# New assumed times in the planner that orders the first batch of an attention and MoE kernel

## The chip, the cores and the metric

The kernel runs on one core of one Trainium2 chip. The metric is the device time of one execution in microseconds; executions of one kernel lie within about half a per cent of their median.

Engine names in the profile: PE is TensorE, PEld its weight loads, ACT is ScalarE, DVE is VectorE, POOL is GpSimd, SP is SyncE.

## The reference

Eight batches of attention with a bias that depends on the distance of query and key, then one MoE-like block on the result:

```python
# q, k, v: (8, 8, 576, 64); bias_table: (32, 8); w_in: (512, 2048); w_out: (2048, 512)
scores = q @ k.T / sqrt(64) + bias[head, bucket(|i - j|)]
attn   = exp(scores - max) / sum            # softmax
x      = (attn @ v), heads side by side     # (4608, 512)
h      = x @ w_in
g      = h + sin(alpha * h)**2 / (alpha + 1e-9)
out    = g @ w_out                          # float32
```

## The kernel before

The kernel does not emit instructions in source order. It describes its work as tasks, each with its engines, an assumed length, its dependencies and an earliest time `nb`. A list scheduler then plays the program through with these assumed times, and emits each task at the moment at which it "starts" in that play. The assumed times therefore decide the *order* of instructions on each engine, and nothing else: on the chip every engine waits on semaphores for its real inputs. Its core:

```python
def ready(self, t):
    r = t.nb                                  # assumed earliest time
    ...                                       # + ends of dependencies, + buffers that come free
def run(self, t0):
    ...
    for t in todo:                            # cut: windows, priorities
        st = max(free[e], self.ready(t))
    ...                                       # the earliest start wins
    t.emit(e)                                 # the instruction is written HERE, in this order
    t.end, t.eng = fin + LAT[e], e
```

The constants that stand for measured times, in us:

```python
T_M2 = (16.8, 20.0)    # landing of the bias factors "m2r" (first head pair, other pairs)
T_MH = (18.0, 18.0)    # landing of the tail factors "mhr"
T_TR1 = (33.0, 37.0)   # landing of "nat", the staged keys and queries of the second batch
T_W = 30.0             # w_in
```

The first batch works on four head pairs p = 0 to 3. For each: scores on PE (`qk`), exponentials on ACT (`ex`), multiplication by the bias factors on DVE (`bd`, `bh`), the products with v on PE (five groups of nine products), normalising on DVE (`norm`), a transpose on PE (`turn`) and a copy into `xT` (`put`, on DVE or ACT). When all four pairs are in `xT`, the first MoE block starts with its sines on ACT. For the second batch, keys and queries are transposed on PE from the staged copy `nat`:

```python
def plan_tr(t, p, kq, pri, nb, deps=()):
    def mm(e):
        c.v = bank("moE").bitcast(F16)
        ...                                   # 12 transposes that read nat2[:, kq, h, ...]
    m = plan.add({"PE": 0.4 if t == 0 and p == 0 else 0.5}, mm, deps, pri, nb, new=[b])
...
if t == 0:
    for p in range(NP):
        for kq in range(2):
            tr[(1, p, kq)] = plan_tr(1, p, kq, 20000 + 100 * kq + 10 * p, T_TR1[kq])
```

The loads come from POOL's queue, in a fixed order that the planner does not touch:

```python
load_m2r(P_, 0, 2)
load_mhr(P_)
cast_v(0, P_, (0, 1))
load_m2r(P_, 2, H)
load_w_in16((0,))
cast_v(0, P_, (2, 3, 4, 5))
load_w_in16((1, 2, 3))
for kq, src in ((0, k), (1, q)):
    load_nat(nat2[:, kq], 0, H, src[1], P_)   # nat
load_v32(1, P_)
load_w_out16()
```

The softmax here doesn't subtract the row's maximum and nothing guards it: scores larger than these inputs give would overflow.

## Time and profile before

| | before |
|---|---|
| time, 6 executions | median 392.96 us (392.29 to 393.67) |
| profiled execution, span | 392.2 us |
| PE busy | 378.4 us, 96% |
| last exponential of the first batch ends | 33.5 us |
| first sine starts | 39.09 us |
| second batch's table load (exponentials may start) | 55.78 us |

The page of the kernel before, its part on busy engines:

```profile
PE 378.4 (96%) x3401; PEld 190.1 (48%) x3401; DVE 262.0 (67%) x587; ACT 323.9 (83%) x458; POOL 81.9 (21%) x96
```

The windows view of the kernel before; each line is one stretch (start:end, length), then busy time of PE, PEld, DVE, ACT and POOL, the granted clock of PE, the DMA share and GB/s.

```profile
22.72:26.13 3.41, 2.00 (x22) 1.21 (x24) 3.35 (x11) 2.63 (x4) 2.63 (x3) 1.00 1.07 211
26.13:29.54 3.41, 3.41 (x46) 2.40 (x46) 2.22 (x7) 2.25 (x4) 0.88 (x1) 0.50 1.06 214
20.00:41.00 21.00, 18.00 (x281) 12.11 (x281) 14.36 (x49) 14.79 (x21) 10.11 (x15) 0.92 1.12 211
57.00:80.00 23.00, 22.99 (x302) 13.30 (x302) 15.80 (x45) 22.18 (x31) 5.57 (x4) 1.00 1.94 166
```

From 57 to 80 us PE is full, and the same view gives it 237.95 busy us of the 240 us from 80 to 320. Nearly all slack is in the first batch, and there one stretch of 3.41 us ran at half clock. Part of the chain of waits of the kernel before (start, length, what):

```profile
15.74 6.42 DMA m2r<-e_dram
22.16 0.02 issue
22.18 0.42 DVE u L730
...
23.36 0.34 PE am L822 x3
```

The second head pair's bias factors land late, DVE starts on them at 22.18, and the first transpose of PE (L822) waits behind DVE. This is what the change aims at. PE's timeline of the kernel before where the first batch ends (start, length, engine, line, operation, output and inputs, shapes, count, and in brackets the idle time ahead with what ended it):

```profile
34.04 0.29 PE L822 MATMUL ca<-id_sb,xn 128*128 128x128 f16 x2 [0.25 <-DVE xn L785]
34.30 0.22 PE L450 MATMUL am<-vh,u 128*128 128x130 f16 x1
...
35.80 0.81 PE L450 MATMUL sc<-xT,w_in 128*128 128x512 f16 x3
...
39.63 0.45 PE L558 MATMUL am<-id_sb,nat 96*64 96x96 f16 x12
```

The last pair's products with v (`am<-vh,u`) start at 34.30, the MoE block's products (`sc<-xT,w_in`) at 35.80, and the first transposes of `nat` come at 39.63, long after `nat` has landed. ACT's timeline of the same stretch:

```profile
33.55 1.28 ACT L937 ACT_TABLE_LOAD   x1
...
39.09 1.84 ACT L865 ACTIVATE s<-sc,alphaT 128x512 f16<-128x512 f32 x3 [1.18 <-PE sc L450]
...
55.78 1.28 ACT L937 ACT_TABLE_LOAD   x1
```

From 39.09 to 55.78 us ACT is full with the block's sines and squares.

### The profile page before, as it was taken

To read this page: it belongs to the slowest core of one execution; us is meant where nothing else is said; L and a number is where in the kernel's file an instruction comes from. 1 tells how busy PE (TensorE), PEld (TensorE's weight loads), DVE (VectorE), ACT (ScalarE), POOL (GpSimd) and SP (SyncE) were. 2 spreads that over 40 slices of the span, in tenths; PEclk is the share of its full clock that TensorE was granted. 3 is DMA by queue.
4 is the path that set the end of the run, shared out by engine and by line. 5 is a ranking of instruction groups with operands and counts; after the bars stand their busy time and mean duration, and the time that the engine had idled before them with its cause. 6 is when DMAs were issued, how large, how long until landed. Compare 5 with 4: busy or idle time off the path is not lost.

```text
span 392.2 us, 8566 instructions
## 1 busy us (share of the span) xinstructions
PE 378.4 (96%) x3401; PEld 190.1 (48%) x3401; DVE 262.0 (67%) x587; ACT 323.9 (83%) x458; POOL 81.9 (21%) x96
## 2 busy tenths in 40 slices
PE   6989999999999999999999999999999999999995
PEld 2456445644455554445445544554445444444442
DVE  3576987768576689567967895768676869429100
ACT  2976999979899999999989999999999969539211
POOL 5762963090004545001700310000000000000000
PEclk9989999999999999999999999999999999999999
DMA  9999999999726999991996497211014000020122
GB/s 170 211 204 219 207 171 158 166 171 148 92 59 83 158 155 157 158 166 47 150 170 101 34 93 166 68 33 42 27 43 59 17 28 29 27 80 2 57 76 80
DMA packets 148647, 41.99 MB, mean 107 GB/s; under 512 B 137784, under 2 KB 142992, under 8 KB 148608
## 3 DMA queue, kind: packets, MB, share of 16 engines
q0 software_dynamic: 89872, 19.04, 56.9%
q1 hardware_dynamic: 58512, 22.36, 30.3%
q8 instruction: 26, 0.43, 0.5%
q14 instruction: 13, 0.11, 0.1%
q10 hardware_dynamic: 224, 0.05, 0.1%
HBM read 37.76 MB, written 16.52 MB: 138 GB/s over the span
## 4 chain that ended last, share of the span: by engine, by line
PE 86%; DMA 4%; DVE 4%; ACT 3%; POOL 1%; issue 1%; ACTq 0%; DVEq 0%
PE sc L450 41%; PE am L450 34%; PE cb L450 5%; PE ca L450 5%; ACT u L705 2%; DMA m2r<-e_dram 2%; DMA e_dram<-e_sb 1%; DMA phi_sb<-phi_const 1%; DVE g L879 1%; DVE u L730 1%; ACT s L865 1%; DVE xn L785 1%; DVE outs L538 0%; DVE kT L538 0%; POOL mhr L471 0%
## 5 line engine op out<-in xcount | busy, mean ns | idle before, releaser
L705 ACT ACTIVATE u<-sc 128x1024 f16<-128x1024 f32 (+1 forms) x192 | 157.8, 898 | 14.4 <-PE sc L450 12.9
L450 PE MATMUL sc<-xT,w_in 128*128 128x512 f16 x576 | 132.3, 379 | 0.6 <-DVE g L879 0.5
L879 DVE SCALAR_TENSOR_TENSOR g<-sq,inv_a,sc 128x512 f16<-128x512 f16 x144 | 103.3, 746 | 22.1 <-PE am L450 14.7
L450 PE MATMUL am<-w_out,g 128*128 128x512 f16 x416 | 108.6, 380 | 0.3 <-DVE outs L538 0.2
L865 ACT ACTIVATE s<-sc,alphaT 128x512 f16<-128x512 f32 x144 | 92.7, 678 | 6.4 <-PE sc L450 5.0
L730 DVE TENSOR_TENSOR u<-u,m2r 128x512 f16<-128x512 f16 (+2 forms) x160 | 67.7, 438 | 32.4 <-ACT u L705 27.8
L450 PEld LDWEIGHTS <-w_in 128*128 128x128 f16 x576 | 55.3, 98 | 65.0 <-issue 1.3
L450 PEld LDWEIGHTS <-g 128*128 128x128 f16 x576 | 53.3, 98 | 64.1 <-issue 11.6
L450 PEld LDWEIGHTS <-u 128*128 128x128 f16 x1440 | 55.8, 98 | 19.2 <-issue 11.0
L450 PE MATMUL sc<-qT,kT 64*128 64x64 f16 (+1 forms) x512 | 50.8, 297 | 1.7 <-ACT u L705 0.9
L450 PE MATMUL am<-v,u 128*128 128x65 f16 x1152 | 51.2, 194 | 0.0
L872 ACT ACTIVATE sq<-s 128x512 f16<-128x512 f16 x79 | 49.2, 628 | 2.2 <-DVE g L879 0.5
L396 POOL DMA_DIRECT2D v<-in_v_dram x24 | 22.2, 1065 | 119.6 <-PE am L450 104.3
L874 DVE TENSOR_TENSOR sq<-s 128x512 f16<-128x512 f16 x65 | 27.4, 423 | 9.2 <-ACT s L865 8.8
L450 PE MATMUL am<-vh,u 128*128 128x130 f16 x144 | 32.2, 224 | 0.8 <-DVE xp L785 0.8
L450 PEld LDWEIGHTS <-kT 64*128 64x128 f16 x512 | 14.7, 96 | 28.5 <-issue 24.3
L785 DVE TENSOR_TENSOR xp<-am,rd 128x384 f16<-128x384 f32 (+1 forms) x48 | 23.6, 491 | 1.8
L784 DVE RECIPROCAL rd<-am 128x6 f32<-128x6 f32 (+1 forms) x56 | 10.5, 187 | 19.7 <-PE am L450 19.2
L450 PE MATMUL cb<-w_out,g 128*128 128x512 f16 x96 | 23.0, 380 | 0.0
L937 ACT ACT_TABLE_LOAD x13 | 16.7, 1283 | 0.2
L377 POOL DMA_DIRECT2D staged_q<-in_q_dram x6 | 15.5, 2583 | 3.6 <-DMA staged_q<-in_q_dram 3.6
L538 DVE COPY outs<-am 128x512 f32<-128x512 f32 x19 | 13.1, 688 | 4.3 <-PE am L450 4.1
(88 smaller groups left out, 175.6 us busy)
## 6 DMA issues: line engine op xcount, KB each, us to landing
out_dram<-outs SPq DMA_DIRECT2D x36, 256.0 KB, 2.2
staged_k<-in_k_dram POOLq DMA_DIRECT2D x6, 576.0 KB, 13.8
staged_q<-in_q_dram POOLq DMA_DIRECT2D x6, 576.0 KB, 19.7
v<-in_v_dram POOLq DMA_DIRECT2D x24, 128.0 KB, 7.0
w_in<-in_moe_w_in_dram POOLq DMA_DIRECT2D x4, 512.0 KB, 8.8
w_out<-in_moe_w_out_dram POOLq DMA_DIRECT2D x4, 512.0 KB, 10.7
w_out<-in_v_dram SPq DMA_DIRECT2D x4, 256.0 KB, 8.2
v1st<-in_v_dram POOLq DMA_DIRECT2D x4, 256.0 KB, 16.6
```

The lines of the kernel that those rows point to most:

```text
L377: nc.gpsimd.dma_start(out=dst.ap()[t].rearrange("s (h d) -> s h d", h=H), in_=src[t].rearrange("h s d -> s h d"),)
L396: nc.gpsimd.dma_start(out=vs[t % 2][:, c, :, 0:D], in_=vp[128 * c : 128 * c + 128],)
L450: nc.tensor.matmul(out=out, lhsT=lhsT, rhs=rhs, start=start, stop=stop)
L538: k_of(e).tensor_copy(out=o, in_=i)
L705: nc.scalar.activation(out=o, in_=x, func=AF.Exp, scale=0.125)
L730: nc.vector.tensor_tensor(out=io, in0=io, in1=m2[:, 2 * p : 2 * p + 2, x0 : x0 + hi - lo], op=ALU.mult,)
L785: nc.vector.tensor_tensor(out=y.rearrange("p c (z d) -> p c z d", z=2), in0=a[:, :, :, 0:D], in1=r.unsqueeze(3).to_broadcast([128, nq, 2, ...
L865: nc.scalar.activation(out=s16.v, in_=h.v, func=AF.Sin, scale=alphaT[:, f : f + 1])
L872: nc.scalar.activation(out=sq.v, in_=s16.v, func=AF.Square)
L874: k_of(e).tensor_tensor(out=sq.v, in0=s16.v, in1=s16.v, op=ALU.mult)
L879: nc.vector.scalar_tensor_tensor(out=gcell[b].v[:, f, :], in0=sq.v, scalar=inv_a[:, f : f + 1], in1=h.v, op0=ALU.mult, op1=ALU.add,)
L937: nc.scalar.preload_act_table_set(name)
```

## The change

Its intent is to plan the first batch with what was measured: later landing of the bias tables, the doubled length of the very first score products, the longer first bias factors, and alpha ready at 12 us. Only assumed times change, and the computation stays the same. The new plan still moves three copies from DVE to ACT and adds one warm-up product on zeros (3402 instead of 3401 on PE).

```diff
 WARM_END = 30.0
+COLD = 1.9
...
-T_M2 = (16.8, 20.0)
-T_MH = (18.0, 18.0)
+T_M2 = (18.0, 20.5)
+D_M2 = (0.25, 0.1)
+T_MH = (18.4, 18.4)
 T_V = (18.5, 45.0)
+T_ALPHA = 12.0
...
-        m = plan.add({"PE": 0.1}, mm, [], 5000, nb=20.0, new=[b])
+        m = plan.add({"PE": 0.1}, mm, [], 5000, nb=T_ALPHA, new=[b])
...
             dur = sum(0.25 if i == "t" else 0.15 if i == 4 else 0.225 for _, i in g)
+            if t == 0 and g[0][0] == 0:
+                dur *= COLD
...
-            done[(w, cc)] = plan.add({"DVE": 0.1 + (hi - lo) / 960.0}, bd, [x], base + 10,
+            more = 0.0 if t else D_M2[p > 0]
+            done[(w, cc)] = plan.add({"DVE": 0.1 + more + (hi - lo) / 960.0}, bd, [x], base + 10,
```

What it does to PE's order at the end of the first batch, as the built program has it (before, from the timeline above: turn, products with v, MoE products, ..., transposes of `nat`):

```
 2 transposes  ca    <- xn                 (third pair's turn)
12 transposes  cb    <- nat2               (second batch, keys, first pair)
 3 products    sc    <- xT, w_in           (first MoE products)
45 products    am/ca <- v, u               (fourth pair's products with v)
```

## The prediction

> **What bounds the kernel now.** The page's first part gives TensorE 378.4 of 392.2 us (96%); the windows view gives it 22.99 of 23.00 us from 57 to 80 us. Beyond the first batch the kernel is a queue on TensorE. Slack exists before: in the first batch's exponentials (9.8 to 33.6 us in the timeline) ScalarE idles about 3.5 us. The chain of waits runs there through the band table: issue at 15.74, landing 6.42 us later, second head pair's first factor at 22.18. Behind it a transpose waits 0.97 us for VectorE, and from 26.13 to 29.54 the granted clock is 0.50, so 512-column products step 0.40 instead of 0.22 us. (The Trainium skill, "TensorE: Matmul & The Clock Gate", Part 1, says that TensorE falls to half rate after an idle window of about 3.4 us; the trace agrees in length, 3.41 us, though the window before had 2.00 us busy.) In the stage of the first sines, 39.09 to 55.78 us, ScalarE is full.
>
> **What the change does.** It alters only times that the planner assumes. No work goes away; one warm-up product is added. In the new order:
> - The alpha transpose and its three VectorE steps (0.65 us) move from 31.2 to about 13 us. That costs about 0.2 us early and frees VectorE later.
> - The third head pair's first scores come before the first attention products; I expect its first exponential near 20.9 instead of 21.35, the fourth pair's near 27.0 instead of 28.29, the last exponential finished near 32.4 instead of 33.5. Three copies of transposed blocks go to ScalarE in between.
> - But TensorE's new order puts the first key transposes of the second batch (12, reading the staged "nat") and three MoE products ahead of the fourth pair's attention products. The planner assumes "nat" at 33.0 us. The trace shows it at about 34.9 us (GpSimd's wait for it ends at 35.2), and GpSimd's order is unchanged. TensorE is in order, so it will stand about 3 us, from near 32 to 34.95.
>
> Walking that order with the trace's lengths: transposes to 35.4, three products to 36.05, five attention groups (1.5) to 37.5, normalise, turn, copy; first sine near 40.2 instead of 39.09. The sine stage has the same ScalarE work (16 sines, 8 squares, 4 copies), so the second batch's exponentials start near 58.2 instead of 57.07. If the 3 us stand brings the half clock back for 3.4 us, as the trace shows can happen, another 1 to 2 us are lost. Some is taken back: TensorE does output products in the delay and has 12 transposes (0.37 us) less to do.
>
> **Prediction.** A gain of about 1 us in the exponentials, a loss of 2 to 4 us at the stand: net about 1.5 us slower, 394.8 us, range 392.3 to 397.2. Faster by over 2%: 1%; within 2%: 98%; slower by over 2%: 1%.
>
> **What would show it.** Right: last exponential of the first batch ends before 33 us; in the waits, TensorE idles 2 us or more for the DMA of "nat" from in_k; first sine after 39.5 us; half clock somewhere between 33 and 41 us; 57 to 80 us still full. Wrong: no wait for "nat", first sine before 38.6.
>
> **What would make it wrong.** "nat" landing earlier than before; the half-clock window of 26 us vanishing, worth over 1 us; later stages, whose order also shifts, gaining or losing about 1 us by chance.

## The result, and the profile after

The changed kernel takes 396.2 us (median of 6 executions, 395.72 to 397.23) against 392.96. The ratio of the mean of its runs to that of the kernel before in the same rounds is 1.0084, with a 95% interval from 1.0067 to 1.0102; ratios here are always means of runs of the same rounds, so they are not quite the ratio of the medians. Executions over 1.5% slower than the fastest of the same kernel are left out of the means. It is slower by 0.8%.

The page after, busy engines:

```profile
PE 378.4 (96%) x3402; PEld 189.5 (48%) x3402; DVE 261.8 (66%) x584; ACT 325.3 (82%) x461; POOL 82.2 (21%) x96
```

PE is busy for the same time to 0.1 us, so the longer span of this profile comes from waiting. This does not say that the clock cost nothing: both profiles hold one later stretch of 3.41 us at half clock, and its slow products count as busy. PE's waits of the changed kernel from 9 to 45 us (who <- for what: total us, times, longest):

```profile
PE cb L561 <- DMA nat<-in_k_dram: 2.7, 1, 2.7
PE sc L453 <- ACT u L710: 1.5, 4, 0.5
```

PE's timeline of the changed kernel:

```profile
32.51 0.28 PE L828 MATMUL ca<-id_sb,xn 128*128 128x128 f16 x2 [0.24 <-DVE xn L791]
35.50 0.69 PE L561 MATMUL cb<-id_sb,nat 96*64 96x96 f16 x12 [2.70 <-DMA nat<-in_k_dram]
36.12 1.46 PE L453 MATMUL sc<-xT,w_in 128*128 128x512 f16 x3
37.38 0.32 PE L453 MATMUL am<-vh,u 128*128 128x130 f16 x1
```

The products with v, which started at 34.30 before, start at 37.38. They were not short of inputs, as DVE's timeline of the changed kernel tells:

```profile
33.51 0.22 DVE L735 TENSOR_TENSOR u<-u,m2r 128x128 f16<-128x128 f16 x1
39.13 0.20 DVE L790 RECIPROCAL rd<-am 128x6 f32<-128x6 f32 x1 [5.40 <-PE am L453]
```

The last factor is done at 33.73; then DVE has nothing to do for 5.40 us. PE stands at the transposes of `nat` although work that it could do lies right behind them. The Trainium skill ("TensorE: Matmul & The Clock Gate", Part 2, step-by-step) says that products stay in program order and only weight loads are pulled ahead; this trace agrees, with 2.70 us of standing. The windows view after (columns as before):

```profile
31.95:35.37 3.42, 0.61 (x9) 0.26 (x5) 1.74 (x7) 2.35 (x4) 0.62 (x1) 1.00 1.30 202
35.37:38.78 3.41, 3.28 (x38) 2.34 (x39) 0.00 (x0) 0.65 (x1) 0.78 (x2) 0.50 1.17 244
57.00:80.00 23.00, 22.99 (x272) 12.19 (x271) 16.70 (x44) 22.88 (x32) 4.40 (x2) 1.00 1.98 156
```

After 3.42 us with 0.61 us of PE work, the granted clock is 0.50 for the 3.41 us in which PE must catch up. From 57 us on, PE is full as before. ACT's timeline of the changed kernel:

```profile
33.04 1.28 ACT L943 ACT_TABLE_LOAD   x1
...
42.17 1.84 ACT L871 ACTIVATE s<-sc,alphaT 128x512 f16<-128x512 f32 x3 [0.53 <-PE sc L453]
...
59.36 1.28 ACT L943 ACT_TABLE_LOAD   x1
```

The first sine comes 3.08 us later than before, the second batch's table load 3.58 us later. The chain of waits now runs through `nat`:

```profile
21.60 13.86 DMA nat<-in_k_dram
35.46 0.04 issue
35.50 0.69 PE cb L561 x12
```

### The profile page after: what moved, and what is told of

Its sections match the earlier page's. It is cut to its first block, busy times and chain, and to the rows that moved or that the text cites. A ratio compares the mean times of both kernels' runs of the same rounds, so it can differ in the third digit from the quotient of the medians.

```text
span 394.6 us, 8568 instructions
## 1 busy us (share of the span) xinstructions
PE 378.4 (96%) x3402; PEld 189.5 (48%) x3402; DVE 261.8 (66%) x584; ACT 325.3 (82%) x461; POOL 82.2 (21%) x96
## 4 chain that ended last, share of the span: by engine, by line
PE 86%; DMA 6%; ACT 3%; POOL 2%; DVE 2%; issue 1%; ACTq 0%; DVEq 0%
PE sc L453 42%; PE am L453 33%; PE cb L453 5%; PE ca L453 4%; DMA nat<-in_k_dram 4%; ACT u L710 2%; DMA e_dram<-e_sb 1%; DMA phi_sb<-phi_const 1%; POOL v L419 1%; POOL w_in L434 1%; ACT s L871 0%; POOL m2r L467 0%; PE cb L561 0%; DVE g L885 0%; DVE outs L541 0%
```

## The experiments

Theory A: the whole loss is the stand at `nat`, made of a wait and of the half clock that follows it. Rivals: B, other parts of the change hurt (early alpha steps, copies moved to ACT, the later stages' order); C, the order itself is harmful even with its data present. All runs gave correct results.

| run | edit, from | median us | ratio to before, 95% | PE's wait for `nat` | first sine |
|---|---|---|---|---|---|
| after | the change | 396.2 | 1.0084 (1.0067 to 1.0102) | 2.70 | 42.17 |
| e1_nat_time | `nat` planned at its landing, after | 392.75 | 0.9995 (0.9978 to 1.0012) | none | 38.14 |
| e2_no_lengths | no factor lengths, after | 391.9 | 0.9982 (0.9958 to 1.0005) | none | 38.27 |
| e4_nat_early | `nat` loaded earlier, after | 392.61 | 0.9998 (0.9975 to 1.0022) | 0.96 | 38.03 |
| e5_warm_stand | PE busy in the stand, after | 394.39 | 1.0031 (1.0013 to 1.005) | 1.37, after 2.3 of filler | 41.68 |
| e3_only_lengths | factor lengths alone, before | 396.32 | 1.0084 (1.0055 to 1.0113) | 3.67 | 43.57 |
| e6_all_undone | control: order of before | 393.18 | 1.0005 (0.9984 to 1.0026) | none | 38.20 |
| e7_only_alpha | alpha alone, before | 393.01 | 1.0014 (0.9988 to 1.004) | none | 37.89 |
| e8_only_landing | landing times alone, before | 392.93 | 1.0003 (0.9978 to 1.0029) | none | 37.94 |
| e9_band_first | e1 and earlier band load | 392.23 (five runs) | 0.9985 (0.9958 to 1.0012) | slow profile | slow profile |
| e10_band_first_alpha | same, fewer lengths | 393.33 | 0.9993 (0.9968 to 1.0017) | none | 38.30 |

### Tell the planner when `nat` really lands

```diff
-T_TR1 = (33.0, 37.0)
+T_TR1 = (35.5, 38.5)
```

> The changed kernel with one number more corrected: the planner is told that the staged copy nat lands at 35.5 and 38.5 us instead of 33.0 and 37.0. Theory A (the loss is the stand at nat, which the new order put ahead of the fourth pair's attention products): TensorE's 2.7 us wait for nat from in_k is gone, the first sine comes near 37.9 us instead of 42.17, and the time is 391.5 to 392.8 us, at or a little below the kernel before (about 393.0). Theory B (other parts of the change hurt: the early alpha steps, three copies moved to ScalarE, or the later stages' order): the wait is gone but the time stays above 394.5 us.

Measured: 392.75 us. PE's waits from 9 to 45 us in this run name no DMA at all:

```profile
PE sc L453 <- ACT u L710: 1.5, 4, 0.5
PE cb L561 <- DVE kT L541: 1.0, 2, 0.6
PE ca L828 <- DVE xn L791: 0.2, 1, 0.2
PE sc L453 <- DVE g L885: 0.2, 1, 0.2
```

The first sine is at 38.14. Everything else of the change is still in, so one line of assumed times accounts for the whole loss. B does not fall by this run alone, since the new times also shift the order of later tasks; it falls with `e4_nat_early` below, which keeps the order. The gain that the change meant does not appear either: the interval leaves room for at most 0.9 us (0.0022 x 393).

### Take the factor lengths out

```diff
-D_M2 = (0.25, 0.1)
+D_M2 = (0.0, 0.0)
```

> The changed kernel without the longer factor lengths in the plan (the lengths added to the first batch's factors set back to zero), all else as changed. The built order no longer has the key transposes of the second batch ahead of the fourth pair's attention products. Theory A: no wait for nat over 1 us, first sine near 38.0 us, time 391.8 to 393.2 us. Theory B: time stays above 394.5 us, since the landing times, the first products' lengths and the alpha move are all still in.

Measured: 391.9 us, first sine at 38.27, no wait for `nat`. As A says. The interval reaches 1.0005, so this is not a shown gain over the kernel before.

### Keep the order, bring `nat` earlier

```diff
-    load_w_in16((1, 2, 3))
-    for kq, src in ((0, k), (1, q)):
-        load_nat(nat2[:, kq], 0, H, src[1], P_)
+    load_w_in16((1, 2))
+    load_nat(nat2[:, 0], 0, H, k[1], P_)
+    load_w_in16((3,))
+    load_nat(nat2[:, 1], 0, H, q[1], P_)
```

> The changed kernel with TensorE's order as it is, but the load of nat's key half issued before the last quarter of w_in instead of after it, so nat should land near 33 instead of 35.5 us. Theory A: the order does no harm once its data are there: the wait for nat shrinks from 2.7 to under 0.6 us, no half clock after it, first sine near 38.3 us, time 391.8 to 393.2 us. Theory C (it is the order itself: transposes and three MoE products ahead of the attention products delay the chain even without a wait): the first sine is still after 39.3 us and the time above 394 us.

Measured: 392.61 us. In the traces the instructions of PE, DVE and ACT stand in the order of the changed kernel, from the first to the last; only POOL's loads differ. PE has its data 2.65 us earlier:

```profile
31.61 0.28 PE L829 MATMUL ca<-id_sb,xn 128*128 128x128 f16 x2 [0.24 <-DVE xn L792]
32.85 0.45 PE L562 MATMUL cb<-id_sb,nat 96*64 96x96 f16 x12 [0.96 <-DMA nat<-in_k_dram]
33.23 0.82 PE L453 MATMUL sc<-xT,w_in 128*128 128x512 f16 x3
33.89 0.22 PE L453 MATMUL am<-vh,u 128*128 128x130 f16 x1
```

A wait of 0.96 us is left, more than expected, because PE arrived 0.9 us earlier in this execution. The clock over 20 to 41 us is 1.00 and the first sine is at 38.03. C falls: the order costs nothing that these runs can see when `nat` is there. B falls too, because every other part of the change, and the order of the later stages, is in this run as it was in the changed kernel.

### Split the stand into wait and clock

Ten products on zeros go into the bank that the transposes will overwrite, just ahead of them:

```diff
-            c.v = bank("moE").bitcast(F16)
+            x_ = bank("moE")
+            if t == 1 and p == 0 and kq == 0:
+                for _ in range(10):
+                    full(x_, zz[:, 0:128], zz, True, True)
+            c.v = x_.bitcast(F16)
```

> The changed kernel with 10 products on zeros (about 2.2 us) put into TensorE's stand just ahead of the transposes that wait for nat, so that TensorE stays busy while it waits. The wait for nat itself ends at the same time, 35.5 us. If the half clock after the stand costs what the trace suggests (1.5 us on the way to the first sine), the granted clock stays 1.00 from 33 to 41 us, the first sine moves from 42.17 to about 40.6 us and the time to 394.3 to 395.3 us. If the half clock costs nothing that counts, the time stays at 395.7 to 396.7 us.

Measured: 394.39 us. PE's timeline:

```profile
32.80 2.32 PE L453 MATMUL cb<-zz 128*128 128x512 f16 x10
36.50 0.45 PE L565 MATMUL cb<-id_sb,nat 96*64 96x96 f16 x12 [1.37 <-DMA nat<-in_k_dram]
36.88 0.82 PE L453 MATMUL sc<-xT,w_in 128*128 128x512 f16 x3
37.54 0.22 PE L453 MATMUL am<-vh,u 128*128 128x130 f16 x1
```

The three MoE products take 0.82 instead of 1.46 us: the clock stayed at 1.00, as the windows view tells:

```profile
20.00:41.00 21.00, 17.81 (x280) 11.55 (x279) 11.66 (x37) 14.88 (x22) 9.69 (x14) 1.00 1.11 199
```

The first sine, at 41.68, missed the expected 40.6, because `nat` landed 1.0 us later in this execution (transposes at 36.50 instead of 35.50). From the start of the transposes to the first sine it took 41.68 - 36.50 = 5.18 us, against 42.17 - 35.50 = 6.67 in the changed kernel: 1.49 us less, the size expected. The run with `nat` early, also at full clock and with the same order, took the same: 38.03 - 32.85 = 5.18 us. In time, the ratios give (1.0084 - 1.0031) x 393 = 2.1 us for the half clock and (1.0031 - 0.9995) x 393 = 1.4 us for the wait. The two groups were timed in different rounds and each interval is about 0.7 us wide to each side, so a difference of two is uncertain by about 1 us and the split is rough; that both parts count is shown.

The half clock was not an accident of one execution. One such stretch lowers the mean clock of a 394.6 us span by 0.5 x 3.41 / 394.6 = 0.004. Some records also hold the half clock of the start (13.65 us in the profiled execution after, 0.017 of the mean), and the last few us, at 0.50 too, take up to 0.002; so the mean is 0.998 to 1.00 or near 0.982 without a later stretch. The six executions of the changed kernel have 0.977, 0.978, 0.995, 0.978, 0.991 and 0.974, each too low by one or two stretches; the six with filler have 0.998, 1.0, 0.983, 1.0, 0.999 and 0.983. Of the 33 executions of the kernel before that were timed beside the experiments, four show such a stretch (0.978, 0.993, 0.994, 0.996).

The traces also tell when the clock fell. Its changes lie on a grid: in the profile before at 26.13, 29.54 and 391.36 us, which is 1 and 106 steps of 3.413 us. With PE's busy time counted on that grid, from 19 us on in the eleven fast profiles (1195 stretches), every stretch with 2.00 us or less was followed by half clock (0.61 in the changed kernel, 1.01 in e3, 2.00 before, and the idle ends of the runs), and every stretch with 2.04 us (the filler run, from 34.09 us) or more by full clock. So in these runs the limit lies between 2.00 and 2.04 busy us of 3.41, as the profile counts them. Where a wait falls on the grid matters as well: in e2 PE waited 2.1 us for DVE across two stretches, which kept 2.42 and 2.27 busy us, and the clock stayed at 1.00.

### Each part of the change alone

```diff
 # e3, from the kernel before:
+D_M2 = (0.25, 0.1)
 # e7, from the kernel before:
+T_ALPHA = 12.0
 # e8, from the kernel before:
-T_M2 = (16.8, 20.0)
-T_MH = (18.0, 18.0)
+T_M2 = (18.0, 20.5)
+T_MH = (18.4, 18.4)
```

> The kernel before with one part of the change alone: the longer factor lengths (0.25 and 0.1 us) in the plan; landing times, first products' lengths and alpha as before. Its built order puts key transposes of the second batch (24 of them, two groups) ahead of the fourth pair's attention products. Theory A: that alone brings a TensorE wait for nat of about 3 us and a time of 395 to 397.5 us. Theory B (the loss comes from another part or from their sum): within 1 us of the kernel before.

Measured: 396.32 us, the whole loss from this part alone. PE's waits:

```profile
PE cb L561 <- DMA nat<-in_k_dram: 3.7, 1, 3.7
PE sc L453 <- ACT u L710: 2.8, 10, 0.5
```

> The kernel before with one part alone: the alpha transpose and its three VectorE steps planned from 12 instead of 20 us. No stand at nat in its order. Theory A: harmless, 392.0 to 393.3 us, within 0.6 us of the control. If the early VectorE steps hurt: the fourth tail's exponential starts over 0.5 us later than in the control and the time is above 393.8 us.

Measured: 393.01 us, first sine at 37.89. Harmless, and no gain.

> The kernel before with one part alone: the measured landing of the band tables (18.0, 20.5 and 18.4 instead of 16.8, 20.0 and 18.0 us). No stand at nat in its order. Theory A: 392.2 to 393.4 us, within 0.6 us of the control, so that none of the change's parts brings a gain of 1 us and the lengths alone bring the loss. If the landing times are worth what the change meant: under 392.0 us.

Measured: 392.93 us, first sine at 37.94. Harmless, and no gain. The fourth part, the doubled length of the first products (`COLD`), was not run alone; it is in e1 and e2, which show no loss.

### A control, and what it says of the profile before

All new numbers set back; the order is that of the kernel before.

> The changed kernel's text with every new number set back; its instruction order is that of the kernel before. A control: 392.3 to 393.7 us. Its profile also tells whether the half-clock stretch at 26 us in the profile before was the rule. Theory A says that it was an accident of that execution (the recorded mean clocks of most other executions leave no room for it): no half clock between 20 and 41 us, first sine near 38.2 us rather than 39.09. If it is the rule: half clock again near 26 us and first sine near 39.

Measured: 393.18 us. The windows view of the control:

```profile
20.00:41.00 21.00, 18.64 (x301) 12.93 (x299) 15.80 (x51) 15.83 (x24) 8.68 (x12) 1.00 1.12 206
```

Its timeline of ACT:

```profile
38.20 1.84 ACT L871 ACTIVATE s<-sc,alphaT 128x512 f16<-128x512 f32 x3 [1.18 <-PE sc L453]
...
54.83 1.28 ACT L943 ACT_TABLE_LOAD   x1
```

The traces of PE, DVE, ACT and POOL have the same instructions in the same order as before. With that order there is no half clock between 20 and 41 us (the profile before had 0.92 there), the last exponential ends at 32.68 instead of 33.53, and the first sine is at 38.20 instead of 39.09. The half clock is where the two part: the last exponential ahead of it started 0.32 us earlier in the profile before (26.54 against 26.86), the next one 0.41 us later (28.29 against 27.88). So 0.9 us of what the profile before showed is put down to one execution's half clock.

### A search for a version that beats both

Both runs issue the second band load right after the first, and plan with `T_M2 = (18.0, 20.0)`, `T_MH = (20.0, 20.0)` and `T_TR1 = (35.5, 38.5)`:

```diff
     load_m2r(P_, 0, 2)
+    load_m2r(P_, 2, H)
     load_mhr(P_)
     cast_v(0, P_, (0, 1))
-    load_m2r(P_, 2, H)
```

> A search for a version that beats both: the change with nat's time corrected as in the first experiment, and the second band-table load issued right after the first, ahead of the tail table and the casts, with the plan told so (band tables at 18.0 and 20.0, tail table at 20.0). If the landing of the second band table is what the exponentials of the first batch wait for: it lands near 20.3 instead of 21.9 us, the first sine comes near 37.3 instead of 38.14 us and the time to 391.3 to 392.3 us. If it is not: same as the first experiment, 392.4 to 393.1 us.

> The same earlier issue of the second band table and nat's corrected time, but with the old lengths in the plan (neither the first products' nor the factors' lengths), alpha early. Walking its order with the trace's lengths puts the first sine about 1 us before that of the kernel before without a half clock (38.20): near 37.1 us, and the time at 391.2 to 392.3 us. If lengths in the plan matter for the gain, it is slower than the run beside it.

Measured: 392.23 us for the first, the median of five runs (its profiled execution, 435.42 us at a clock of 0.855, was slow and is not used; with it the median is 392.69), and 393.33 us for the second. Neither is distinguishable from the kernel before. In the second the band table landed at 21.2 us, not near 20.3, and its first sine was at 38.30, not 37.1. Both expectations of a gain missed.

## Why the prediction was right or wrong

- *The stand.* Right. "It will stand about 3 us, from near 32 to 34.95": it stood 2.70 us, from 32.8 to 35.5. The landing was 0.5 us later than in the profile before.
- *The exponentials' start times.* Right within 0.5 us. The third pair's first exponential was at 21.08 (20.9 predicted), the fourth pair's at 27.45 (27.0), and the last one ended at 32.64 (32.4).
- *The first sine.* Predicted near 40.2, measured 42.17. Of the 1.97 us between, 0.5 us is the later landing, and 1.49 us is the half clock, which the filler run measured.
- *The half clock.* Foreseen in size ("another 1 to 2 us") but carried as an "if". It came in all six executions. Here the walk to the first sine, which left it out, was too short.
- *"A gain of about 1 us in the exponentials."* Wrong, and this is the term of the sum that failed. The 1 us was counted against a profile whose half clock at 26 us was not the rule. Against the control, the last exponential ends at 32.64 instead of 32.68. That these two agree is partly luck, since the second band table landed at 21.36 and at 20.79 us; over all fast profiles this end lies between 31.73 and 33.93. The time is the better evidence: with the stand removed, the first sine is at 38.14 against 38.20, and the time ratio is 0.9995. The change has no gain that these runs can see. The prediction listed this half clock among what could make it wrong, but as a possible further gain of the changed kernel.
- *What is given back.* Right in kind. Against the control, the second batch's table load is 59.36 - 54.83 = 4.53 us late, and ACT's last table load, for the last sines, 302.10 - 298.88 = 3.22 us late. So 1.3 us are taken back in between; from 57 to 80 us PE stays full (22.99 of 23.00 us). Which of the named works gives them back is not shown.
- *The total.* "Net about 1.5 us slower, 394.8 us": measured 3.2 us slower, 396.2 us, inside the stated range. The loss put at the stand, 2 to 4 us, holds the measured 3.2 us without any gain, so the main mis-sized term is the gain (1 put, none found); the half clock, weighed as possible, was in every execution of the changed kernel (1.5 us on the way to the first sine). The range was wide enough to hold an unchanged time of 392.96 too, so it tests the mechanism less than the wait and the first sine do.

Why the lengths bring the stand can be read from the plan. The factors that the fourth pair's first product waits for end at 33.66 us in the changed plan, against 32.27 before and 31.95 without the lengths (e2). So PE seems idle from 32.63 us, and the planner puts there what is "ready" at 33.0 us, the transposes of `nat`. With the new time of e1 they are planned at 38.68 us, behind the product at 34.02. The number for `nat` had been wrong by 2 us before as well. It did no harm while the plan had other work in that place.

What stays open is whether the run without factor lengths, at 391.9 us, is really 0.2% faster than the kernel before; its interval includes no difference.

## What to carry to other kernels

When a scheduler works from assumed times, correct them together: correcting some made the plan rely on one that was still wrong, and an in-order engine turns such an error into a stand that all work behind it shares. Put work that reads a DMA behind work whose data are surely there, or assume its landing late; `nat` landed at 34.9 us in the profile before and at 37.4 us in that of the control, whose instructions are the same in the same order. And before counting a gain against one profile, look whether that profile holds an accident, such as a stretch at half clock, that other executions lack.

## What the Trainium skill lacked or had wrong

- "TensorE: Matmul & The Clock Gate", Part 1, table of the two states: it gives the half clock after an idle window. Here windows that were not idle preceded it, with PE busy 2.00 of 3.41 us (before) and 0.61 of 3.42 us (after). No share of busy time is stated at which the clock falls; in these traces the limit lies between 2.00 and 2.04 us of 3.41, as the profile counts busy time.
- The same page, "Why this matters for your kernels", advises no gaps over about 3 us. Here a single gap of 2.70 us was followed by the half clock, with a cost of about 1.5 us on the chain to the first sine; in the profile before the longest gap in the stretch was 0.97 us. The busy time within one stretch, and not the length of a gap, parts the cases.
- No page read for this case tells how far a DMA's landing varies between executions of the same program; here `nat` landed at 34.9 us (before) and 37.4 us (control, the same instructions in the same order).
